# Six chunks' scores on 40 rows instead of 104, a mask moved to GpSimd, and a new order of the first steps: an mLSTM with a feed-forward on one core

## The chip, the cores and the metric

The kernel runs on one NeuronCore of one Trainium2 chip. TensorE multiplies matrices, VectorE (DVE), ScalarE (ACT) and GpSimd (POOL) do elementwise work, and SyncE (SP) issues nearly all DMAs. The metric is the device time of one execution in microseconds: 464.96 us is the median of three runs (464.77 to 465.43).

## The reference

An mLSTM over 768 time steps for 4 batches and 8 heads of width 40, then a feed-forward of width 2048 over the heads' joined outputs (3072 tokens of 320):

```python
for t in range(S):
    m_new = np.maximum(f_gate[:, :, t] + m, i_gate[:, :, t])
    f_stab, i_stab = np.exp(f_gate[:, :, t] + m - m_new), np.exp(i_gate[:, :, t] - m_new)
    C = f_stab * C + i_stab * outer(vt, kt);  n = f_stab * n + i_stab * kt;  m = m_new
    y[:, :, t] = sigmoid(o_gate[:, :, t]) * (C @ qt) / np.maximum(np.abs(n @ qt), 1.0)
h = x @ w_in
out = (np.maximum(h, 0) + alpha * np.minimum(h, 0)) @ w_out
```

## The kernel before, in words

The 768 steps of a batch are six chunks of 128 tokens; chunk n = 6b + c is chunk c of batch b, 24 in all. Inside a chunk the recurrence is written as attention: scores K Q^T of each head (keys on the partitions, queries along the row) times a decay matrix E that is zero where the key comes after the query, times the values; and what came before the chunk enters through a state C, which is multiplied by a decay gamB and added to for each chunk (`update`, lines 183 to 223). Two chunks are one group g of 256 tokens, 12 groups, on which the feed-forward runs: `up_steps` (lines 749 to 787) multiplies by w_in, `down` (789 to 813) by w_out, in eight pairs fp of 128-column blocks. The result of a pair is split in a high part (`gh`, ScalarE) and a low part (`gl`); the token letters of a pair are U R S G K, where VectorE computes into PSUM and makes the low part, or V r s g N, where GpSimd makes the low part (line 785).

The weights come as float64. Each block is loaded (token letter d), scaled by ScalarE (s), joined from its two words by VectorE (j), and split in a high part by ScalarE (h, H) and a low part by VectorE (l, L) or by GpSimd (p, P), line 891. The third bit group comes either by ScalarE (x, line 865) with a longer join on VectorE (line 877), or by a shift on VectorE (y, line 871) with another join (line 879).

The first six chunks (batch 0, `n < NDIR`) take a road of their own. q and k are loaded by token, transposed on TensorE (`transposed`, line 266: two heads to a block, head 2p on partitions 0 to 39 and head 2p+1 on 64 to 103, with zeros between) and copied from PSUM by ScalarE. k goes to a padded tile of two halves (`padded_copy`, lines 322 and 323): the half of the even heads has zeros on the partitions from 64, that of the odd heads on those below 64, so that the scores (line 1097) may contract over all 104 partitions:

```python
nc.tensor.matmul(ps[:, sl], qk[n][1][:R, par, sl], qk[n][0][:R, sl], start=True, stop=True)
```

`par` is the parity of the head; a call makes the four heads of one parity, in float32, which the trace shows as two records (a weight load and a matmul each) per instruction. The decays of chunks 0 to 3 come through PSUM: `barred` (line 100) first writes a triangle of large negative numbers with a 512-column bfloat16 matmul, `spread` (1052) or `spread_later` (1064) adds the rows of L to it, and ScalarE takes the exponential (1080). Chunks 4 and 5 load L by DMA, and GpSimd zeroes the upper triangle of E with a select (line 489). VectorE multiplies scores and E (line 1101).

The order of all this is written out by hand: ORDER (line 686) is a string of 414 tokens, each a step with its instructions, and `pin` (line 944) holds every engine's queue to that order. After ORDER's last token Z0 (group 0's output is copied out at 104 us) a repeating PATTERN issues the rest; steps done in ORDER are left out there. A warm token is that many bfloat16 matmuls of 256 columns whose output nobody reads. PSUM tiles named by `psa` come from two tags, "a" and "b", of two buffers each, given in turn.

Of the kernel before, what the change touches and what calls it, by code (L numbers as in the profile page):

```python
# [17 lines left out]
def kernel(ctx: ExitStack, tc: tile.TileContext, q, k, v, i_gate, f_gate, o_gate, w_in, w_out, alpha, out):  # L18
# [286 lines left out]
    kpads = []  # L305

    def padded_tiles():


        for K in kpads:  # L310
            nc.gpsimd.memset(K[64:R, 0], 0.0)
            nc.gpsimd.memset(K[:64, 1], 0.0)

# [102 lines left out]
    def gated_steps(n, hv):  # L416
# [21 lines left out]
        if b == 0:  # L438
            nc.vector.scalar_tensor_tensor(out=sg, in0=sg, scalar=1.0, in1=rb, op0=ALU.add, op1=ALU.mult)
        else:  # L440
            nc.gpsimd.tensor_tensor(sg, sg, rb, ALU.mult)
# [38 lines left out]
    def decays_of(n, par, Lb):  # L480
# [3 lines left out]
        for p in range(NPR):  # L484
            h = 2 * p + par
            nc.scalar.activation(  # L486
                E[:, p * P : (p + 1) * P], Lb[:, h], AF.Exp, bias=bT[:, c, b * H + h : b * H + h + 1]
            )
        nc.gpsimd.affine_select(
# [166 lines left out]
    def first_stacks():  # L656
# [23 lines left out]
    XNP = range(2, NBF)  # L680
    KDP = range(1, 24)
    CP = range(6, 24)
    OBA = range(0)
    WIDE = 3 * VA
    ORDER = """warm18 kfz alT lf0z warm2 warm2 i00d i00s sca0 lf0a lf0b dq0 L0 sp01 qT0 dq1 alC li0 bj0 wt0 bTt kT0 i00x qc0 kc0 ewj
        i01d sca1 bTc ex01 sp00 sc00 qT1 wTt eeL wTc qc1 wd0 li1 lf1a lf1b kT1 sc01 i00j ex00 kc1 eTt Cz eTc sp11 ex11
        dv0 wg01 i01s wd1 L1 um0 uc0 i01x lpa um1 sp10 wg00 gma gmd ex10 i01j i00h fm1 ft1 sc11 do0 sc10 wg10 bj1 wtl
        blt ewl blc i00p o0d o0s r0d o0x gmm gmc r0s r0x v0 wg11 lpb lpc lpd uc1 dq2 qT2 o2d gr0 wlt og1 warm2 wlc r0j
        i11d lpe o0j i01h i01p gg0 qc2 dq3 gx0 gp0 kT2 v1 eel elt elc sp21 kc2 sc21 dL r0H ta1 gr1 gg1 sp20 ex21 qT3
        wg21 i10d dv1 r0h gx1 gp1 r0p r0L ex20 wd2 sc20 wg20 qc3 x0 x1 xa0 xd0 dq4 fm2 wd3 xa1 xd1 i10s F0 ft2 o2s o2y  # L690
        sp31 o0h ex31 kT3 o2j o2h i10y i10j um2 U00 o0l V01 kc3 R00 i11s uc2 i11y i11j o2l do1 i10h i10l sp30 r01 qT4
        qc4 ex30 S00 v2 sc31 i20d i20s ta2 gr2 i20x wg31 o1d og2 gg2 gx2 kT4 i20j kc4 sc30 wg30 G00 K00 i21d fm3 ft3
        s01 i20h o1s i20p i11h i11p o1x r2d o1j i21s i21x sc41 v3 um3 i21j uc3 ta3 dL4 U02 V03 r2s r2y o3d gr3 sc40
        ex41 fm4 R02 dq5 o1h o1l o4d g01 r2j N01 qT5 i21h i21p o3s S02 o3x G02 K02 dL5 wg41 i31d ft4 D00 wd4 dq6 o3j
        qc5 dv2 r2h r2p r03 ex40 o4s r2H D01 o4x gg3 s03 o3h o4j gx3 o5d gp3 wg40 i30d V04 r04 s04 dv3 o4h V05 gp2 x2
        x3 xa2 xd2 o6d do2 wd6 kT5 g04 r2P g03 o3l xa3 r05 o4l s05 v4 xd3 kc5 i31s ta4 N03 N04 i31y i31j i30s o5s o5x
        F1 V10 gr4 r10 um4 uc4 dL6 i30x um6 U11 ex50 R11 o5j s10 uc6 S11 ex51 g10 i31h dL7 i31p sc50 N10 i30j dq7 wg50
        U12 fm5 ft5 o5h sc51 wg51 v5 o7d R12 S12 ta5 D10 G11 K11 o6s o6x gr5 og3 gg5 G12 gx5 gg4 D11 K12 D12 i30h i30l
        gx4 U13 gp5 D02 tp0 do3 U06 o7s gp4 o5l o6j vp0 R13 tp1 g05 S13 G13 N05 K13 o7x o6h D13 vp1 o7j U07 tp2 tp3
        R06 S06 R07 x4 x5 xa5 xd5 D03 D04 D05 S07 o7h o7l G06 K06 o6l D06 xa4 xd4 G07 K07 D07 Z0"""  # L700
# [36 lines left out]
    class FeedForward:  # L737

        def __init__(self, g):
            self.g, self.x, self.done, self.named = g, x_tiles.pop(g), [], 0  # L740
# [4 lines left out]
        def up(self):  # L745
            for step in self.up_steps(self.g < 2):
                pass

        def up_steps(self, split=True):
            g, fp = self.g, self.named  # L750
            self.named += 1
# [34 lines left out]
            self.done.append((gh, gl))  # L786
# [179 lines left out]
    def first_group():  # L966
# [79 lines left out]
        def spread(n, par):  # L1046

            pb = psa(f"pb{n}_{par}")
            barred(pb)
            for p in range(NPR):  # L1050
# [3 lines left out]
                    start=False, stop=p == NPR - 1  # L1054
# [3 lines left out]
        def spread_later(n, par):  # L1058

            pb = psa(f"pb{n}_{par}")  # L1060
            barred(pb)
            for p in range(NPR):
# [3 lines left out]
                    LP[:, n % GC * P : (n % GC + 1) * P], start=False, stop=p == NPR - 1,  # L1066
# [5 lines left out]
        def decay(n, par):  # L1072
# [10 lines left out]
            E[n, par] = e  # L1083
# [4 lines left out]
        def scores(n, par):  # L1088
            if n >= GC:
                ps = psa(f"pS{n}_{par}")  # L1090
            elif n * par == 0:
# [275 lines left out]
```

## Time and profile before

| | us |
|---|---|
| median of three runs (range) | 464.96 (464.77 to 465.43) |
| the profiled execution, whole | 465.35 |
| its span, first to last instruction | 463.6 |
| TensorE busy in the first 80 us | 72.75 |
| TensorE busy from 80 to 450 us | 370.00 of 370 |
| DVE, ACT, POOL busy in the first 80 us | 65.93, 66.71, 45.05 |

The profiled execution has 1.7 us outside its span. Busy time of TensorE counts a matmul from its start to its modelled end, while the next may have begun: where matmuls follow each other, the step from start to start is shorter than the duration shown, and a short wait can lie inside busy time.

### The profile page before, as it was taken

The page shows a single profiled execution, that of the slowest core. Times are in us where ns is not written, and L with a number is a line of the kernel's source. Part 1 is how long each engine was busy: PE and PEld are TensorE (multiplying, and loading weights), DVE is VectorE, ACT ScalarE, POOL GpSimd, SP SyncE. Part 2 cuts the span into 40 slices and gives each one's busy share as a digit, 9 for nine tenths or more (in the row PEclk, how much of TensorE's full clock was granted, in tenths as well). Part 3 has the DMA queues.
Part 4 walks back from the last instruction along what each step waited for, and adds up shares of the span by engine and source line. Part 5 has one row for each costly group of instructions (what it writes and reads, how often), then busy time and mean ns, then how long its engine had stood idle before and what let it go on. Part 6 is the DMA issues. An engine that isn't in the chain of part 4 may idle for free.

```text
span 463.6 us, 11813 instructions
## 1 busy us (share of the span) xinstructions
PE 452.8 (98%) x4366; PEld 442.0 (95%) x4366; DVE 329.8 (71%) x692; ACT 315.0 (68%) x707; POOL 308.4 (67%) x377
## 2 busy tenths in 40 slices
PE   8989989999999999999999999999999999999996
PEld 6879978999999999999999999999999999999996
DVE  4989998747776787886875887886776786764321
ACT  4899898676857858758856958757857858423331
POOL 8551674854698697588888598588888686324231
PEclk9999999999999999999999999999999999999999
DMA  9999994869775775888997686688796463020000
GB/s 184 177 221 252 277 252 118 175 122 190 151 182 147 138 184 160 137 174 173 158 187 176 122 197 168 133 166 180 153 206 156 107 154 90 1 84 15 28 2 28
DMA packets 186306, 68.67 MB, mean 148 GB/s; under 512 B 150234, under 2 KB 178506, under 8 KB 186250
## 3 DMA queue, kind: packets, MB, share of 16 engines
q1 hardware_dynamic: 186170, 67.83, 67.2%
q8 instruction: 34, 0.56, 0.5%
q14 instruction: 22, 0.18, 0.2%
q10 hardware_dynamic: 80, 0.11, 0.1%
HBM read 40.44 MB, written 7.57 MB: 104 GB/s over the span
## 4 chain that ended last, share of the span: by engine, by line
PE 83%; DVE 5%; DMA 5%; SPq 3%; ACT 3%; issue 1%; ACTq 0%; DVEq 0%
PE po L796 36%; PE ph L759 5%; PE ph L765 5%; PE ph L762 5%; PE ph L760 5%; PE ph L761 5%; PE ph L764 4%; PE ph L763 4%; PE ph L766 4%; PE pH L377 4%; PE pS L515 4%; DMA wi<-in_moe_w_in_dram 2%; DMA wr<-in_moe_w_in_dram 2%; PE pI L403 1%; PE pu L203 1%; DMA qn<-in_q_dram 1%
## 5 line engine op out<-in xcount | busy, mean ns | idle before, releaser
L785 POOL TENSOR_TENSOR gl<-g,gh 128x512 fp32r<-128x512 f32 x77 | 100.5, 1306 | 42.9 <-ACT gh L783 39.6
L796 PE MATMUL po<-OH,gh 128*128 128x320 f32 x368 | 110.7, 312 | 0.0
L796 PE MATMUL po<-OL,gh 128*128 128x320 f32 x368 | 109.3, 309 | 0.0
L769 ACT ACTIVATE g<-ph 128x512 f32<-128x512 f32 x96 | 57.1, 596 | 58.2 <-PE ph L766 56.0
L774 DVE SCALAR_TENSOR_TENSOR g<-g,oma,ph 128x256 f32<-128x256 f32 x156 | 66.8, 469 | 32.7 <-ACT g L769 32.3
L796 PEld LDWEIGHTS po<-OL,gh 128*128 128x128 f32 x368 | 69.2, 188 | 0.1
L796 PEld LDWEIGHTS po<-OH,gh 128*128 128x128 f32 x368 | 69.1, 188 | 0.0
L796 PE MATMUL po<-OH,gl 128*128 128x320 f32 x368 | 69.0, 309 | 0.0
L759 PE MATMUL ph<-XH,WH 128*128 128x256 f32 x192 | 57.2, 298 | 1.1 <-ACT wo L865 0.7
L796 PEld LDWEIGHTS po<-OH,gl 128*128 128x128 f32 x368 | 57.9, 188 | 0.0
L764 PE MATMUL ph<-XL,WH 128*128 128x256 f32 x192 | 54.3, 283 | 0.9 <-DVE XL L623 0.9
L765 PE MATMUL ph<-XL,WH 128*128 128x256 f32 x192 | 54.3, 283 | 0.0
L762 PE MATMUL ph<-XH,WL 128*128 128x256 f32 x192 | 54.3, 283 | 0.0
L760 PE MATMUL ph<-XH,WH 128*128 128x256 f32 x192 | 54.1, 282 | 0.0
L761 PE MATMUL ph<-XH,WL 128*128 128x256 f32 x192 | 54.1, 282 | 0.0
L364 ACT CAST E<-pS 128x512 bf16<-128x512 f32 x72 | 41.6, 582 | 18.0 <-DVE pS L361 14.0
L763 PE MATMUL ph<-XH,W 128*128 128x256 f32 x192 | 53.4, 278 | 0.2 <-POOL W L891 0.2
L766 PE MATMUL ph<-XL,W 128*128 128x256 f32 x192 | 53.4, 278 | 0.0
L783 ACT CAST gh<-g 128x512 fp32r<-128x512 f32 x77 | 46.5, 618 | 9.1 <-DVE g L774 6.6
L486 ACT ACTIVATE E<-Lb,bT 128x128 f32<-128x128 f32 x160 | 50.0, 392 | 0.0
L361 DVE TENSOR_TENSOR pS<-pS,E 128x512 f32<-128x512 f32 x36 | 24.8, 690 | 29.6 <-PE pS L515 26.2
L759 PEld LDWEIGHTS ph<-XH,WH 128*128 128x128 f32 x192 | 36.1, 188 | 2.0 <-ACT wo L865 0.9
(197 smaller groups left out, 1123.2 us busy)
## 6 DMA issues: line engine op xcount, KB each, us to landing
Lb<-L_d SPq DMA_DIRECT2D x20, 512.0 KB
wo<-in_moe_w_out_dram SPq DMA_DIRECT2D x8, 640.0 KB
wi<-in_moe_w_in_dram SPq DMA_DIRECT2D x8, 512.0 KB
qn<-in_q_dram SPq DMA_DIRECT2D x24, 160.0 KB
kn<-in_k_dram SPq DMA_DIRECT2D x24, 160.0 KB
va<-in_v_dram SPq DMA_DIRECT2D x24, 160.0 KB
og<-in_o_gate_dram SPq DMA_DIRECT2D x24, 160.0 KB
out_dram<-ob SPq DMA_DIRECT2D x11, 320.0 KB
```

The costliest lines, as they stand in the source:

```text
L759: nc.tensor.matmul(dst, WH[half][:, 0, hs], XH[:, 0], start=True, stop=False)
L760: nc.tensor.matmul(dst, WH[half][:, 1, hs], XH[:, 1], start=False, stop=False)
L761: nc.tensor.matmul(dst, WL[half][:, 0, hs], XH[:, 0], start=False, stop=False)
L762: nc.tensor.matmul(dst, WL[half][:, 1, hs], XH[:, 1], start=False, stop=False)
L763: nc.tensor.matmul(dst, W2[:, fs], X2, start=False, stop=False)
L764: nc.tensor.matmul(dst, WH[half][:, 0, hs], XL[:, 0], start=False, stop=False)
L765: nc.tensor.matmul(dst, WH[half][:, 1, hs], XL[:, 1], start=False, stop=False)
L766: nc.tensor.matmul(dst, W2[:, fs], X2L, start=False, stop=True)
L769: nc.scalar.activation(gt, ph, AF.Relu, scale=-1.0)
L774: nc.vector.scalar_tensor_tensor(out=y[:, e], in0=gt[:, e], scalar=oma[:, f : f + 1], in1=ph[:, e], op0=ALU.mult, op1=ALU.add)
L785: (nc.vector if split else nc.gpsimd).tensor_tensor(gl, y, gh.bitcast(F32), ALU.subtract)
L796: nc.tensor.matmul(po[j], x[:, e, j * P : (j + 1) * P], W[f // NB][:, f % NB], **ends)
```

## The change

- `scores(n)` makes both parities in one call. Each head is a matmul over its own 40 partitions (0 to 39 or 64 to 103), even and odd heads in turn, into two PSUM tiles. k is then copied unpadded, in one ScalarE copy instead of two, and the four memsets of the padded tiles (token kfz) are gone.
- Chunk 3 is taken out of the barred chunks (BAR): its spread begins the PSUM group itself, and GpSimd's select masks E.
- CP: for chunks 1 to 4, GpSimd multiplies C by its decay, in one instruction of 104x336, where VectorE did it in two. KDP: chunk 1's weighted keys go to VectorE. XNP: chunk 1's last gating product goes to GpSimd and chunk 2's to VectorE. OGP is empty: its steps (tokens ga) issue nothing, and `gated_steps` is as before.
- ORDER is new throughout, with 419 tokens. By its tokens: four low parts of w_out go from VectorE to GpSimd (ol 8 to 4, op 0 to 4) and one of the w_in rest (rL to rP); five blocks go from x to y (two of w_in, three of w_out); four feed-forward pairs go from U to V (00, 07, 11, 13); warm2 three times is now warm3 three times. The DMAs are the same, in another order (q of chunk 0 is now first on SP).
- The first 50 PSUM tiles without a tag take theirs from a written list.

```diff
+    first_turns = list("abababaaabbbaabbabbbaaababbaababababbabaaaabbbbbaba")
     def psa(name, tag=None):
+        if tag is None and first_turns:
+            tag = first_turns.pop(0)
...
-    XNP = range(2, NBF)
-    KDP = range(1, 24)
-    CP = range(6, 24)
+    XNP = (1, *range(3, 6))
+    KDP = range(2, 24)
+    CP = range(1, 24)
+    OGP = range(0)
+    BAR = range(3)
...
-    ORDER = """warm18 kfz alT lf0z warm2 warm2 i00d i00s sca0 lf0a lf0b dq0 L0 sp01 qT0 dq1 alC li0 bj0 wt0 bTt kT0 i00x qc0 kc0 ewj
+    ORDER = """dq0 warm18 qT0 i00d dq1 lf0z alT sca0 qc0 sca1 lf0a lf0b li0 alC i00s do0 L0 kT0 i00x warm3 eeL sp01 bj0 bTt
...
-        R06 S06 R07 x4 x5 xa5 xd5 D03 D04 D05 S07 o7h o7l G06 K06 o6l D06 xa4 xd4 G07 K07 D07 Z0"""
+        D05 o6l K06 xd5 g07 xa4 N07 o7l D06 xd4 D07 Z0"""
...
             if j == 0:
-                qk[n] = sb.tile([P, 512], F32, tag="qf", name=f"qf{n}"), padded(n)
-                copy(qk[n][j][:R], pq[:R])
-            else:
-                padded_copy(qk[n][j], pq)
+                K = sb.tile([P, 2, 512], F32, tag="kS", name=f"kf{n}", bufs=2)[:, 0]
+                qk[n] = sb.tile([P, 512], F32, tag="qf", name=f"qf{n}"), K
+            copy(qk[n][j][:R], pq[:R])
...
-            barred(pb)
+            if n in BAR:
+                barred(pb)
...
-            E[n, par] = e
+            E[n, par] = e if n in BAR else causal(e)
...
+            for h in range(H):
+                p, par = divmod(h, 2)
+                sl, r = slice(p * P, (p + 1) * P), slice(64 * par, 64 * par + D)
+                nc.tensor.matmul(pS[n, par][:, sl], qk[n][1][r, sl], qk[n][0][r, sl], start=True, stop=True)
...
-                steps[f"sc{n}{par}"] = lambda par=par: scores(n, par)
+                steps[f"sc{n}{par}"] = lambda: (n, 0) in pS or scores(n)
```

## Rows read from the trace of the kernel before

**Rows 1.** Busy time by stage: the window in us, its length, then busy us (and instructions) of PE, PE's weight loads, DVE, ACT and POOL, the granted TensorE clock, the DMA engines' mean busy share and GB/s.

```profile
0.00:80.00 80.00, 72.75 (x655) 66.17 (x656) 65.93 (x137) 66.71 (x148) 45.05 (x65) 1.00 0.93 211
80.00:450.00 370.00, 370.00 (x3644) 366.04 (x3644) 261.33 (x551) 245.08 (x555) 260.81 (x311) 1.00 0.65 139
...
30.00:40.00 10.00, 9.64 (x96) 8.69 (x95) 8.88 (x20) 9.40 (x24) 3.43 (x4) 1.00 0.84 159
...
70.00:80.00 10.00, 8.94 (x77) 8.42 (x72) 8.15 (x18) 8.15 (x20) 4.85 (x6) 1.00 0.36 105
```

**Rows 2.** What TensorE waited for, whole span, the longest waits behind the one for the constants at the start: its line, the releaser's engine, tile and line, us in total, times, longest.

```profile
PE ph L764 <- DVE XL L623: 0.9, 1, 0.9
PE pb L100 <- DVE xn L443: 0.8, 1, 0.8
PE pH L337 <- DVE E L1101: 0.8, 2, 0.6
PE ph L759 <- ACT wo L865: 0.7, 1, 0.7
PE ps_gw L1022 <- ACT E L1080: 0.5, 1, 0.5
PE ps_ge L1022 <- ACT g_WH L1227: 0.4, 1, 0.4
```

**Rows 3.** The chain that ended last, in order of time: start us, us, what; one DMA issue on SP (SPq) at its start, and its two longest transfers of weights.

```profile
2.20 0.58 SPq L106
...
14.25 8.14 DMA wr<-in_moe_w_in_dram
...
37.39 8.24 DMA wi<-in_moe_w_in_dram
```

**Rows 4.** TensorE's timeline from 14 to 22 us: start us, us from the first start to the last end, engine, line, operation, tiles, shape, and how many records follow each other.

```profile
13.63 0.39 PE L100 MATMUL pb<-later,ident 128*128 128x512 bf16 x1
13.86 1.05 PE L1052 MATMUL pb<-g_L,ident 128*128 128x128 f32 x8
14.84 0.81 PE L203 MATMUL pu<-va,kd 128*40 128x42 f32 x32
15.59 0.39 PE L100 MATMUL pb<-later,ident 128*128 128x512 bf16 x1
```

**Rows 5.** TensorE's timeline from 9 to 11.5 us (the scores of one parity, eight records), and line 1097 as a whole: durations ns min/median/max, first and last start.

```profile
9.77 1.06 PE L1097 MATMUL pS<-qf,kf 104*128 104x128 f32 x8
...
L1097 PE MATMUL pS<-qf,kf x96: 272/275/377, 9.8 to 77.4; 104*128 104x128 f32 x96
```

**Rows 6.** Line 203, the state's update, as a whole: the same columns.

```profile
L203 PE MATMUL pu<-va,kd x320: 199/202/233, 14.8 to 379.3; 128*40 128x42 f32 x160
```

**Rows 7.** Groups of DVE in the first 80 us, shapes apart: line, operation, out<-in, shapes, count | busy us, mean ns | idle before.

```profile
L877 DVE SCALAR_TENSOR_TENSOR t_wo<-t_wo,wo 128x640 uint32<-128x640 uint32 x5 | 5.7, 1140 | 0.4 <-ACT wo L865 0.2 <-POOL xn L443 0.2
L877 DVE SCALAR_TENSOR_TENSOR t_wi<-t_wi,wi 128x512 uint32<-128x512 uint32 x5 | 4.6, 923 | 0.0
L891 DVE TENSOR_TENSOR OL<-t_wo,OH 128x640 fp32r<-128x640 f32 x5 | 4.0, 810 | 0.0
L221 DVE TENSOR_TENSOR C<-C,gamB 40x168 f32<-40x168 f32 x8 | 2.5, 318 | 0.1
L879 DVE SCALAR_TENSOR_TENSOR t_wi<-wi,t_wi 128x512 uint32<-128x512 uint32 x3 | 2.1, 692 | 0.1
L871 DVE TENSOR_SCALAR t_wi<-t_wi 128x512 uint32<-128x512 uint32 x3 | 1.7, 574 | 0.0
L785 DVE TENSOR_TENSOR gl<-ph,gh 128x512 fp32r<-128x512 f32 x2 | 1.4, 686 | 0.7 <-ACT gh L783 0.7
L879 DVE SCALAR_TENSOR_TENSOR t_wo<-wo,t_wo 128x640 uint32<-128x640 uint32 x1 | 0.8, 828 | 0.0
L871 DVE TENSOR_SCALAR t_wo<-t_wo 128x640 uint32<-128x640 uint32 x1 | 0.5, 494 | 0.4 <-ACT t_wo L855 0.4
```

**Rows 8.** The same view of ACT.

```profile
L323 ACT COPY kf<-pqk 40x512 f32<-40x512 f32 x6 | 3.5, 581 | 0.1
L865 ACT ACTIVATE wo<-wo 128x640 uint32<-128x640 uint32 x5 | 4.0, 802 | 0.0
L865 ACT ACTIVATE wi<-wi 128x512 uint32<-128x512 uint32 x5 | 3.4, 676 | 0.0
```

**Rows 9.** The same view of POOL.

```profile
L891 POOL TENSOR_TENSOR WL<-t_wi,WH 128x512 fp32r<-128x512 f32 x6 | 8.2, 1371 | 1.6 <-ACT WH L887 1.5
L785 POOL TENSOR_TENSOR gl<-g,gh 128x512 fp32r<-128x512 f32 x3 | 4.9, 1660 | 2.3 <-ACT gh L783 2.3
L172 POOL TENSOR_TENSOR kd<-kn,wT 128x320 f32<-128x320 f32 x5 | 3.5, 719 | 0.1
L489 POOL TENSOR_SCALAR_AFFINE_SELECT E<-E 128x512 f32<-128x512 f32 x4 | 2.7, 679 | 6.8 <-ACT E L486 4.1 <-DVE C L221 2.3 <-POOL W L891 0.4
L443 POOL TENSOR_TENSOR xn<-T,og 128x320 f32<-128x320 f32 x2 | 1.9, 972 | 10.5 <-DVE og L439 10.5
```

**Rows 10.** The spread of one instruction's duration on DVE, by line: ns min/median/max, first and last start us.

```profile
L877 DVE SCALAR_TENSOR_TENSOR t_wo<-t_wo,wo x7: 826/1291/1583, 24.7 to 90.6; 128x640 uint32<-128x640 uint32 x7
L439 DVE SCALAR_TENSOR_TENSOR og<-og,r x6: 483/492/1553, 25.9 to 82.3; 128x320 f32<-128x320 f32 x6
L891 DVE TENSOR_TENSOR OL<-t_wo,OH x8: 774/818/1446, 37.2 to 99.8; 128x640 fp32r<-128x640 f32 x8
```

More of the change, by code (lines that the diff above doesn't have):

```diff
@@ L143, in open_gate_last, with open_gate_early @@
         nc.vector.tensor_scalar(og, og, 1.0, None, ALU.add)
+    def open_gate_early(n):
+        if n in OGP:
+            sg = o_tiles[0][:, n]
+            nc.gpsimd.tensor_scalar(sg, sg, 1.0, None, ALU.add)
     def open_gate(b, c0=0, c1=NC):
@@ L303, in shifted @@
         chunk[n] = (Q, K, None)
[L305 to L312, printed above, removed]
     def zero_states():
@@ L438, in gated_steps @@
         if b == 0:
-            nc.vector.scalar_tensor_tensor(out=sg, in0=sg, scalar=1.0, in1=rb, op0=ALU.add, op1=ALU.mult)
+            if n in OGP:
+                nc.gpsimd.tensor_tensor(sg, sg, rb, ALU.mult)
+            else:
+                nc.vector.scalar_tensor_tensor(out=sg, in0=sg, scalar=1.0, in1=rb, op0=ALU.add, op1=ALU.mult)
         else:
@@ L488, in decays_of, with causal @@
             )
+        return causal(E)
+    def causal(E):
         nc.gpsimd.affine_select(
@@ L739, in __init__ @@
         def __init__(self, g):
-            self.g, self.x, self.done, self.named = g, x_tiles.pop(g), [], 0
+            self.g, self.x, self.done = g, x_tiles.pop(g), {}
             if g == 1:
@@ L743, in __init__, with up_steps @@
                 self.po = [ps_a.tile([P, 512], F32, tag="b", name=f"po{g}_{j}")[:, :DM] for j in range(GC)]
[L745 to L751, printed above, removed]
+        def up_steps(self, fp, split):
+            g = self.g
             XH, XL, X2, X2L = self.x
@@ L785, in up_steps @@
             (nc.vector if split else nc.gpsimd).tensor_tensor(gl, y, gh.bitcast(F32), ALU.subtract)
-            self.done.append((gh, gl))
+            self.done[fp] = gh, gl
             yield
@@ L1027, in by_token @@
             yield
-        for j in range(2):
-            kpads.append(sb.tile([P, 2, 512], F32, tag="kS", name=f"kf{j}", bufs=2))
         qk = {}
@@ L1053, in spread @@
                     pb[:, p * P : (p + 1) * P], ident[:, h : h + 1].broadcast_to([P, P]), L_all[:, n * P : (n + 1) * P],
-                    start=False, stop=p == NPR - 1
+                    start=n not in BAR, stop=n not in BAR or p == NPR - 1
                 )
@@ L1060, in spread_later @@
             pb = psa(f"pb{n}_{par}")
-            barred(pb)
+            if n in BAR:
+                barred(pb)
             for p in range(NPR):
@@ L1065, in spread_later @@
                     pb[:, p * P : (p + 1) * P], pick[:, h : h + 1].broadcast_to([3 * BH, P]),
-                    LP[:, n % GC * P : (n % GC + 1) * P], start=False, stop=p == NPR - 1,
+                    LP[:, n % GC * P : (n % GC + 1) * P], start=n not in BAR, stop=n not in BAR or p == NPR - 1,
                 )
@@ L1082, in decay, with scores @@
                 )
-            E[n, par] = e
+            E[n, par] = e if n in BAR else causal(e)
             yield
         pS = {}
[L1088 to L1091, printed above, removed]
-                ps = ps_h.tile([P, 512], F32, tag="h", name=f"pS{n}_{par}")
-            else:
-                ps = ps_o.tile([P, 512], F32, tag="o1", name=f"pS{n}_{par}")
-            for p in range(NPR):
-                sl = slice(p * P, (p + 1) * P)
-                nc.tensor.matmul(ps[:, sl], qk[n][1][:R, par, sl], qk[n][0][:R, sl], start=True, stop=True)
-            pS[n, par] = ps
+        def scores(n):
+            for par in range(2):
+                if n >= GC:
+                    pS[n, par] = psa(f"pS{n}_{par}")
+                elif n * par == 0:
+                    pS[n, par] = ps_h.tile([P, 512], F32, tag="h", name=f"pS{n}_{par}")
+                else:
+                    pS[n, par] = ps_o.tile([P, 512], F32, tag="o1", name=f"pS{n}_{par}")
+            for h in range(H):
+                p, par = divmod(h, 2)
+                sl, r = slice(p * P, (p + 1) * P), slice(64 * par, 64 * par + D)
+                nc.tensor.matmul(pS[n, par][:, sl], qk[n][1][r, sl], qk[n][0][r, sl], start=True, stop=True)
         def weigh(n, par):
@@ L1245, in chunk_steps @@
                 add(f"fm{n} ft{n}", lazily(lambda: state_part(n)))
+            steps[f"ga{n}"] = lambda: open_gate_early(n)
             add(f"gr{n} gg{n} gx{n} gp{n}", lazily(lambda: gated_steps(n, got["T" if n else "h", n])))
@@ L1306, in named_ffn @@
                 for tokens, split in (("URSGK", True), ("VrsgN", False)):
-                    add(" ".join(f"{x}{g}{fp}" for x in tokens), lazily(lambda split=split: ffs[g].up_steps(split)))
+                    add(" ".join(f"{x}{g}{fp}" for x in tokens), lazily(lambda fp=fp, split=split: ffs[g].up_steps(fp, split)))
                 steps[f"D{g}{fp}"] = lambda fp=fp: ffs[g].down(fp)
```

36 lines of the change are left out of this document (16 added, 20 removed).

## The prediction

> **What bounds the kernel now.** The busy time by stage comes first [rows 1]. From 80 to 450 us TensorE is busy for 370.00 of 370 us, with DVE, ACT and POOL at 66 to 71%: there TensorE's own instructions are the time. In the first 80 us it is busy for 72.75 and idle for 7.25, with DVE at 65.93, ACT at 66.71 and the DMA engines at a mean share of 0.93; POOL has 35 us free. So the end comes at: all the work of TensorE, plus the time in which it stands still in the first 80 us. The change can act on these two alone, and nothing that it does on another engine behind 80 us is worth anything.
>
> What TensorE waits for is read next [rows 2]. No single wait is over 0.9 us. Those for DVE (0.9, 0.8, 0.8) make 2.5 us, those for ACT (0.7, 0.5, 0.4) 1.6 us: together 4.1 of the 7.25. The chain that ended last [rows 3] shows what is under them: two transfers of weights stand in it with 8.14 and 8.24 us, so that in part of the first 46 us neither DVE nor ACT sets the pace but the loads. Those are all issued again.
>
> **TensorE's work, part by part.** Scores: eight records of one parity take 1.06 us from first start to last end, and one lasts 0.275 [rows 5], so they follow each other in (1.06 - 0.275) / 7 = 0.112 us. A chunk has 16 records, 1.79 us; six chunks 10.8 us. The change keeps the 96 records and their 128 columns; what it can save is time in which an even head's records run beside an odd head's. Does this chip do that? The trace has no matmul on part of the rows beside another. It has the nearest kin, the state's update, whose even heads write to partitions 0 to 39 and odd ones to 64 to 103: 32 records in 0.81 us, each 0.202 long [rows 4, 6], follow each other in (0.81 - 0.20) / 31 = 0.0196 us. At the scores' rate per column, 42 columns would take 0.112 x 42 / 128 = 0.037 us. The update goes twice as fast, so its heads do run in pairs. If rows behave as columns, a chunk's 16 records in the order even, even, odd, odd need 8.5 slots of 0.112 (the first and the last stand alone): 0.95 us, which saves 0.84 a chunk and 5.0 us in six.
>
> The update also shows what it costs to enter and leave such a mode [rows 4]. The last record before it starts at 13.86 + 1.05 - 0.28 = 14.63, the update at 14.84: 0.21 instead of 0.11. Its own last record starts at 14.84 + 0.81 - 0.20 = 15.45, the next matmul at 15.59: 0.14 instead of 0.02. So a block pays 0.10 + 0.12, and six blocks 1.3 us. The scores give 5.0 - 1.3 = 3.7; I take -3.6, as a feed-forward matmul behind a block may pay a little more. The ends are +1.3 (no pairs, the switches alone) and -5.0 (no switches). The Trainium skill's page "TensorEngine Tiling (Array Packing)", section "Tiling Modes", says that changing the tiling mode drains TensorE; that is the 0.22 us just read, and by it the change pays six drains that the kernel before did not have.
>
> Bars: two matmuls of 512 columns go, with 13.86 - 13.63 = 0.23 us from start to start [rows 4]: -0.46. Warm matmuls: three more of 256 columns, half a bar each: 3 x 0.115 = +0.35; where they fill a wait they cost nothing, so between 0 and that. TensorE's work: -3.6 - 0.46 + 0.35 = -3.7 us.
>
> **What the other engines lose or get in the first stage** (some of it falls behind 80 us, where it counts for nothing). DVE: C's decay, 8 x 0.318 = -2.5; four low parts of w_out, 4 x 0.81 = -3.2; one of the rest, 0.69 by the 512 columns of line 785 = -0.7; four pairs from U to V, 4 x 0.686 = -2.7 [rows 7]. Five blocks from x to y cost it, for w_in, 0.574 + 0.692 - 0.923 = 0.34 twice, and for w_out 0.494 + 0.828 - 1.140 = 0.18 three times: +1.2. Chunk 1's keys: +0.5, as a 128x320 product of two tiles (the shortest of line 439 is 0.483 [rows 10]). The two gating products change places. Sum -7.4 us of 65.9. ACT: six copies of k less, 6 x 0.581 = -3.5, and five third bit groups less, 2 x 0.676 + 3 x 0.802 = -3.8 [rows 8]: -7.3 of 66.7. POOL gets four low parts of 640 columns (1.371 x 640/512 = 1.71 each), one of 512 (1.3), four low parts of pairs (1.66 each), four decays of C (0.72 to 0.97 each by 128x320 products; I take 0.85) and two selects (0.68) [rows 9]: 6.9 + 1.3 + 6.6 + 3.4 + 1.4 = 19.6, less chunk 1's keys (0.7) and four memsets at the start. About 17 us more on 45: some 62 of 80, so it has room.
>
> C's decay now stands ahead of the addition of the new part on another engine: DVE's addition waits for POOL, and behind it stand the next chunk's row scaling and product. As the decay needs only the state before, it can run while the update's matmuls do; I price it at nothing, and at up to 0.8 us a chunk (an instruction of POOL that it meets) if POOL is late. Both parities' scores now want two of four PSUM buffers at once: also nothing, and at most a wait like the 0.8 us of line 100 [rows 2].
>
> The loads keep their sizes and their queue, SP, and change places. At the head, q and k of chunk 0 were issued behind the first block of w_in; now q goes ahead of it. That puts the block back by one issue of some 0.58 us [rows 3], and TensorE's first transpose, now straight behind the 18 warm matmuls, holds the scans' transposes behind it if q is late. Further back, loads of weights, v and gates change places by a few issues each. I price each at nothing, since what they feed is not the next thing in its engine's queue, and at one issue, 0.6 us, for the first block if ScalarE is there early; what the moves do together lies in the idle time below.
>
> **DVE and POOL disturb each other.** Line 877's instruction on the same shape takes 0.826 to 1.583 us, line 439's 0.483 to 1.553, line 891's 0.774 to 1.446 [rows 10], all with two inputs in SBUF. The Trainium skill's page "SBUF — State Buffer", section "Who interferes with whom", has a rule that speaks against this change: a DVE instruction with two SBUF inputs and a GpSimd instruction that reads SBUF hold each other up, the later one for all of the earlier. The spreads agree with it. By the rows alone: with 17/45 more POOL time, a hold-up of up to 0.76 us (1.583 - 0.826) is met more often; I allow 2 us of the 7.4, so that DVE keeps -5.
>
> **TensorE's idle time.** With DVE and ACT 5 to 7 us lighter, the 4.1 us of waits for them may shrink; against that TensorE has 3.7 us less to do, mostly in the stage, and where a load sets the pace this comes back as idle time. I take the balance at -0.8: from -4.1 (all these waits go) to +3.7 (all is given back).
>
> **Sum.** 465.35 - 3.7 - 0.8 = 460.85 for an execution like the profiled one. That lies 0.39 above the median of the runs shown, so the forecast is 460.5 us.
>
> **The rivals.**
> - *The waits go too.* For: DVE and ACT lose 11% each where they were 83% busy. Against: the transfers in [rows 3]. 464.96 - 3.7 - 4.1 = 457.2.
> - *The loads keep the pace.* For: DMA share 0.93 over the stage, only 0.84 from 30 to 40 us and 0.36 from 70 to 80 [rows 1]. Against: TensorE idles 7.25 us and not more, so that loads do not hold it for most of the stage. Then only what is saved behind the last load counts, the scores of chunk 5 (the last records start at 77.4 us [rows 5]): 3.6 / 6 = 0.6, and 464.4.
> - *Rows do not pair.* The change would not do what it says: +1.3 - 0.46 + 0.35 = +1.2 in work, -0.8 in waits: 465.4. Against it speaks the update's rate.
> - *Slower: POOL's new work holds DVE up.* 15 instructions are new on POOL (4 + 1 + 4 + 4 + 2). If 12 of them hold a DVE instruction for 0.76 us, DVE gets 9.1 and loses 7.4: +1.7 in a stage that it then sets, and TensorE's saving is idle time: 466.7. It decides from 10 hold-ups on (7.4 / 0.76). For: of line 877's seven instructions on w_out the middle one already takes 1.291 [rows 10]. Against: part of what moves away from DVE (the low parts of line 891) is itself of the kind that is held up.
>
> **How the numbers follow.** The forecast has 0.55 (458.5 to 462.5), the waits that go too 0.18, the loads 0.08, no pairs 0.06, POOL's hold-up 0.13. A difference under 0.2% (0.93 us) cannot be told from none: the loads and no pairs lie within it, so faster 0.73, same 0.14, slower 0.13. For 8 in 10 the range leaves out the slower case and the far half of the fastest: 456 to 465.5.
>
> **What would show it.** In the changed profile: line 1097's successor as 96 records with 40 rows, 16 of them in about 0.95 + 0.28 us from first start to last end (right) or in 2 us (no pairs); a gap of 0.1 us on both sides of each block; six matmuls of line 100's kind instead of eight; DVE and ACT some 5 to 7 us lighter and POOL some 17 heavier by the end of the first 110 us; TensorE idle for 6 to 7 us in the first 75 us and at 100% from there. The prediction is wrong if idle time in the stage is over 10 us (loads or POOL), if line 877's median rises beyond 1.4 us with TensorE waiting on DVE, or if TensorE saturates as late as before.

## The result, and the profile after

The changed kernel takes 468.10 us (median of four runs, 468.08 to 468.18), the one before 464.87 us in the same comparison: a ratio of 1.0068, with a 95% interval from 1.0054 to 1.0082. It is slower by 3.2 us, where 4.4 us less was forecast, and lies outside the range.

The first view is the busy time by stage of the changed kernel, with the columns of [rows 1]; three shorter windows around one event follow.

```profile
0.00:80.00 80.00, 68.91 (x644) 61.48 (x645) 62.64 (x119) 57.84 (x133) 53.32 (x71) 0.98 0.88 200
80.00:450.00 370.00, 368.61 (x3631) 364.26 (x3630) 262.92 (x556) 247.16 (x557) 265.76 (x314) 1.00 0.65 141
...
55.00:62.40 7.40, 4.90 (x36) 4.40 (x34) 6.86 (x13) 4.11 (x9) 5.28 (x7) 1.00 1.03 320
62.40:65.80 3.40, 3.18 (x15) 3.21 (x16) 2.74 (x5) 3.35 (x9) 1.02 (x3) 0.50 0.55 64
65.80:80.00 14.20, 14.20 (x150) 13.70 (x149) 11.94 (x22) 10.82 (x27) 11.26 (x12) 1.00 0.56 142
```

The whole execution with the same columns, the kernel before first:

```profile
0.00:463.60 463.60, 452.83 (x4366) 442.04 (x4366) 329.80 (x692) 315.04 (x707) 308.45 (x377) 1.00 0.68 148
```

```profile
0.00:466.40 466.40, 450.79 (x4367) 438.75 (x4367) 328.97 (x681) 309.12 (x696) 324.21 (x387) 1.00 0.67 147
```

TensorE stands idle for 11.09 us of the first 80 (7.25 before), and for 1.4 us more behind 80, where it had none. Over the whole span its busy time falls by 2.0 us and its idle time grows from 10.8 to 15.6 us; together these are the 2.8 us between the two spans. The DMA share is 0.88 against 0.93, so the loads do not press harder. In the first 80 us ACT does 8.9 us less and DVE 3.3 us less, but the changed kernel is late there (119 instructions of DVE instead of 137). Over the whole execution ACT does 5.9 us less and DVE only 0.8, although the change takes 7 us from each. POOL does 15.8 us more. And for 3.4 us, behind a wait of TensorE, its granted clock is 0.50, that is 1.2 instead of 2.4 GHz.

The scores themselves do what the update's rows promised. The next fence is TensorE's timeline with one chunk's block, and line 1095 as a whole (what was line 1097 in [rows 5]).

```profile
12.22 1.16 PE L1095 MATMUL pS<-qf,kf 40*128 40x128 f32 x16
13.31 0.65 PE L274 MATMUL pqk<-ident,qn 128*104 128x128 f32 x4
...
L1095 PE MATMUL pS<-qf,kf x96: 272/272/373, 12.2 to 76.6; 40*128 40x128 f32 x96
```

From the block's first start to the next instruction's start the 16 records take 13.31 - 12.22 = 1.09 us, entry and exit partly in it, where they took 1.8.

The waits of the changed kernel, against [rows 2] (the columns as there; TensorE's over the whole span, the two others over the first 90 us):

```profile
PE p L604 <- DVE T L400: 2.5, 1, 2.5
PE pH L329 <- DVE E L1098: 1.4, 1, 1.4
PE pS L1095 <- DVE C L230: 0.9, 1, 0.9
...
DVE C L230 <- POOL C L218: 4.1, 3, 2.2
...
ACT qf L1035 <- PE pqk L274: 6.4, 3, 2.8
ACT gh L780 <- DVE ph L771: 3.3, 1, 3.3
ACT t_wi L852 <- POOL OL L888: 2.0, 2, 1.3
```

```profile
ACT qf L1039 <- PE pqk L266: 1.0, 1, 1.0
```

Each engine now waits for another: TensorE for DVE, DVE for the decays that were moved to POOL, ACT for POOL's low parts and, for 6.4 us, for TensorE's transposes of q. The last line is the kernel before, where that wait was 1.0 us. Of the 6.4 us, 2.8 lie at the very start, where ACT waited 2.7 us for the first block of w_in before; the other 3.6 stand against the 1.0.

Last, DVE and POOL side by side from 76 to 82 us (start, us, engine, line, operation), and DVE's small gating instruction by line:

```profile
77.22 0.64 DVE L1098 TENSOR_TENSOR E<-pS,E 128x512 f32<-128x512 f32 x1
77.77 3.49 DVE L868 TENSOR_SCALAR t_wo<-t_wo 128x640 uint32<-128x640 uint32 x1
...
77.61 0.82 POOL L259 TENSOR_TENSOR C<-cw,C 40x336 bf16<-40x336 f32 x1 [0.58 <-ACT C L257]
78.40 1.27 POOL L782 TENSOR_TENSOR gg<-g,gg 128x512 fp32r<-128x512 f32 x1
79.63 1.28 POOL L782 TENSOR_TENSOR gl<-g,gh 128x512 fp32r<-128x512 f32 x1
...
L422 DVE SCALAR_TENSOR_TENSOR r<-T x5: 166/587/1844, 27.9 to 87.7; 128x8 f32<-128x8 f32 x5
```

A shift of 0.49 us lasts 3.49 us: it ends at 81.26, and three POOL instructions that follow each other without a gap end at 80.91. A 128x8 instruction of 0.17 us lasts up to 1.84: it starts at 56.47 us and ends at 58.32, and the second of two POOL instructions in a row ends at 58.29. In both cases DVE's instruction ends just behind the last of a chain of POOL's.

### The profile page after: what moved, and what is told of

Read it like the earlier page. It is cut to its first block, busy times and chain, and to the rows that moved or that the text cites. A ratio compares the mean times of both kernels' runs of the same rounds, so it can differ in the third digit from the quotient of the medians.

```text
span 466.4 us, 11800 instructions
## 1 busy us (share of the span) xinstructions
PE 450.8 (97%) x4367; PEld 438.8 (94%) x4367; DVE 329.0 (71%) x681; ACT 309.1 (66%) x696; POOL 324.2 (70%) x387
## 4 chain that ended last, share of the span: by engine, by line
PE 86%; DVE 5%; ACT 3%; POOL 3%; issue 1%; DMA 1%; DVEq 0%; POOLq 0%
PE po L793 35%; PE ph L756 5%; PE ph L759 5%; PE ph L762 5%; PE ph L761 4%; PE ph L757 4%; PE ph L758 4%; PE ph L763 4%; PE ph L760 4%; PE pH L369 4%; PE pS L514 4%; PE pH L329 2%; PE pu L211 1%; PE pI L395 1%; POOL WL L888 1%; PE pb L1047 1%
## 5 line engine op out<-in xcount | busy, mean ns | idle before, releaser
L782 POOL TENSOR_TENSOR gl<-g,gh 128x512 fp32r<-128x512 f32 x79 | 103.1, 1307 | 38.3 <-ACT gh L780 35.0
L771 DVE SCALAR_TENSOR_TENSOR g<-g,oma,ph 128x256 f32<-128x256 f32 x164 | 70.2, 469 | 33.8 <-ACT g L766 33.2
L780 ACT CAST gh<-g 128x512 fp32r<-128x512 f32 x79 | 47.8, 617 | 9.0 <-DVE g L771 6.5
L759 PEld LDWEIGHTS ph<-XH,WL 128*128 128x128 f32 x192 | 36.8, 192 | 0.7 <-POOL WL L888 0.7
```

Of the source, the lines that this page charges most:

```text
L759: nc.tensor.matmul(dst, WL[half][:, 1, hs], XH[:, 1], start=False, stop=False)
L771: nc.vector.scalar_tensor_tensor(out=y[:, e], in0=gt[:, e], scalar=oma[:, f : f + 1], in1=ph[:, e], op0=ALU.mult, op1=ALU.add)
L782: (nc.vector if split else nc.gpsimd).tensor_tensor(gl, y, gh.bitcast(F32), ALU.subtract)
```

## The experiments

All times are medians, each beside runs of the kernel before on the same chip (464.8 to 465.1 in all five groups, so that differences between runs of two groups are good to some 0.3 us); the last column is the ratio to it with its 95% interval.

| run | us | ratio |
|---|---|---|
| e1 rows in pairs alone, in the kernel before | 469.0 | 1.008 (1.005 to 1.011) |
| e2 changed, POOL's work back | 468.3 | 1.007 (1.005 to 1.009) |
| e3 changed, POOL's low parts write only | 466.2 | 1.002 (1.001 to 1.003) |
| e4 before, POOL's low parts write only | 464.8 | 0.999 (0.998 to 1.000) |
| e5 e1's places, 104 rows | 467.4 | 1.005 (1.003 to 1.007) |
| e6 e1, waits filled | 465.8 | 1.002 (1.000 to 1.004) |
| e7 changed, rows unpaired | 470.0 | 1.010 (1.009 to 1.012) |
| e8 changed, 104 rows | 472.5 | 1.017 (1.014 to 1.019) |
| e9 changed, waits filled | 468.1 | 1.007 (1.005 to 1.008) |
| e10 changed, decays back | 466.5 | 1.004 (1.002 to 1.005) |
| e11 pairs at the first place, in the kernel before | 466.4 | 1.003 (1.002 to 1.005) |
| e12 changed, low parts back | 466.2 | 1.003 (1.002 to 1.004) |
| e13 changed, decays and low parts back | 467.6 | 1.005 (1.004 to 1.007) |
| e14 changed, feed-forward pairs back | 468.4 | 1.007 (1.005 to 1.008) |
| e15 changed, shifts back | 468.8 | 1.008 (1.006 to 1.009) |
| e16 e11 with warm matmuls | 466.1 | 1.003 (1.001 to 1.004) |
| e17 the new order alone | 474.5 | 1.021 (1.019 to 1.022) |
| e18 before, two low parts on POOL | 465.5 | 1.001 (1.000 to 1.002) |

**The order alone (e17, e8, e7).** These three and the changed kernel make a ladder, and it is the main result. e17 keeps the new order and the work of before. Some of its lines against the changed kernel:

```diff
-    XNP = (1, *range(3, 6))
-    KDP = range(2, 24)
-    CP = range(1, 24)
+    XNP = range(2, NBF)
+    KDP = range(1, 24)
+    CP = range(6, 24)
...
-    BAR = range(3)
+    BAR = range(4)
```

The scores go over 104 rows again, and ORDER has the new places with the tokens of before: o0l o1l o2l o4l r0L, the pairs U00 U07 U13, and x or y for each block as before. The order here also takes in the places of the loads, both parities' scores in one place, and the written list of PSUM tags, which e17 keeps.

> The new order with the work of the kernel before: 104-row scores, chunk 3 barred, decays, keys, gating products, low parts, the forms of the weight blocks and the feed-forward pairs as before (pair 11 alone stays with GpSimd). If the order itself is what costs: 470 to 474, about as much as e8. If the moved work was the loss: 465 to 467.

474.45 us: the order theory's number, half a microsecond above its range. The new order with the old work costs 474.45 - 464.77 = 9.7 us. Where it falls behind is read from the busy time by stage; the first three rows are of the kernel before, the last three of e17 (both have the same instructions, but for one feed-forward pair, two low parts of w_in that change engines against each other, and three warm matmuls):

```profile
0.00:30.00 30.00, 26.17 (x228) 22.24 (x228) 21.36 (x47) 21.84 (x51) 19.21 (x39) 1.00 1.02 207
30.00:60.00 30.00, 29.27 (x266) 27.68 (x265) 27.61 (x54) 27.86 (x62) 13.97 (x13) 1.00 0.98 232
60.00:90.00 30.00, 27.31 (x239) 26.25 (x238) 23.93 (x50) 24.07 (x51) 19.51 (x23) 1.00 0.74 182
```

```profile
0.00:30.00 30.00, 25.61 (x212) 21.33 (x212) 18.99 (x42) 19.14 (x44) 17.68 (x37) 1.00 1.11 210
30.00:60.00 30.00, 26.57 (x241) 24.04 (x239) 21.76 (x48) 24.48 (x55) 8.72 (x10) 1.00 0.76 175
60.00:90.00 30.00, 26.68 (x225) 25.34 (x224) 26.00 (x47) 23.44 (x50) 18.62 (x19) 0.94 0.70 186
```

At 60 us DVE has done 40.75 us of work instead of 48.97, ACT 43.62 instead of 49.70, TensorE 453 records instead of 494. The kernel before keeps DVE and ACT over 90% busy from 30 to 60 us; e17 has them at 73 and 82%. Its waits in the first 90 us name several links:

```profile
ACT qf L1052 <- PE pqk L274: 8.2, 4, 3.0
ACT XH L633 <- DVE XL L638: 1.7, 1, 1.7
...
DVE t_wr L884 <- ACT t_wr L868: 2.9, 1, 2.9
DVE OL L904 <- ACT OH L900: 2.6, 2, 2.5
...
PE p L620 <- DVE T L416: 1.4, 1, 1.4
```

The largest is ACT's for the transposes of q. Its first two waits, what stands ahead of the second in TensorE's queue, and ACT's wait at the start of the kernel before:

```profile
5.97 0.59 ACT L1052 COPY qf<-pqk 104x512 f32<-104x512 f32 x1 [2.96 <-PE pqk L274]
14.67 0.58 ACT L1052 COPY qf<-pqk 104x512 f32<-104x512 f32 x1 [3.00 <-PE pqk L274]
...
12.14 2.05 PE L1114 MATMUL pS<-qf,kf 104*128 104x128 f32 x16
14.03 0.60 PE L274 MATMUL pqk<-ident,qn 128*104 128x128 f32 x4
```

```profile
5.68 0.67 ACT L855 ACTIVATE t_wi<-wi 128x512 f32<-128x512 f32 x1 [2.67 <-DMA wi<-in_moe_w_in_dram]
```

The first wait takes the place of one that the kernel before had too. The other 5.2 us stand against 1.0 in the kernel before: in TensorE's queue the scores or the values of an older chunk stand ahead of the transposes, ACT stands still, and what it makes for DVE comes late. How much of the 9.7 us this link makes was not tried; that the order makes them is measured.

e8 keeps order and moved work, with the scores over 104 rows; e7 keeps the 40 rows but issues the even heads first and then the odd ones:

```diff
-            for h in range(H):
+            for h in (0, 2, 4, 6, 1, 3, 5, 7):
```

> The changed kernel with its order, but the scores over 104 padded rows as before (two copies of k on ScalarE and the memsets of the padded tiles back). Give-back theory: 466.5 to 469.5, with TensorE at the full clock throughout; what the order and the moved work cost, some 3 us, is all there. If TensorE's saved time is worth its length: 471 to 473.

> The changed kernel with the four even heads of a chunk ahead of the four odd ones, so that only one pair of records in 16 can overlap: TensorE has some 4.7 us (6 chunks x 7 slots x 0.112) more to do, all else is the same. Give-back theory: the waits shrink by as much, the time is 466 to 469. If TensorE's saved time is worth its length: 471.5 to 473.

472.54 and 469.95 us. e8 goes against the give-back theory, e7 lies between the two. A block of e7 still overlaps in part:

```profile
12.02 1.71 PE L1095 MATMUL pS<-qf,kf 40*128 40x128 f32 x16
```

It is 0.55 us longer than the changed kernel's, 3.3 us in six. So the moved work gives 474.45 - 472.54 = 1.9 us, and the scores on 40 rows, with ScalarE's single copy of k and without the memsets, 472.54 - 468.10 = 4.4 us, of which 1.9 come from taking even and odd heads in turn instead of all even ones first. The order takes 9.7, the work gives back 6.3. These steps hold in this sequence alone: taken out of the changed kernel one by one, two parts of the moved work cost time (e10, e12 below). The old order with all of the new work was not run.

**The pairs in the kernel before (e1, e5, e6, e11, e16).** e1 takes the new `scores` into the kernel before, with both parities where the later one stood (kfz gone, three weighings behind the scores); e5 has these places with 104 rows; e6 is e1 with matmuls in its waits; e11 has both parities where the first stood and no weighing moved; e16 is e11 with ten more warm matmuls.

```diff
-... sp21 kc2 sc21 dL ... wg21 i10d dv1 ... wd2 sc20 wg20 ...
+... sp21 kc2 dL ... i10d dv1 ... wd2 sc20 wg21 wg20 ...            (e1, e5, e6)
+... sp21 kc2 sc21 dL ... wg21 i10d dv1 ... wd2 sc20 wg20 ...       (e11, e16: sc21 makes both)
+... warm8 v0 ... warm14 v3 ... hold14 U11 ... hold8 v5 ...         (e6)
+... warm6 elt ... warm4 sp21 ...                                   (e16)
```

> The kernel before with the scores by 40 rows and in pairs, nothing else of the change: its own order, its own division between VectorE and GpSimd; a chunk's scores are issued where the later parity's were, and the weighing of three parities follows them. If the pairing is worth on TensorE what the trace after shows (96 records at a mean step of 0.056 us instead of 0.112, less six changes of mode), the time falls by 2.5 to 4.5 us, to 460.5 to 462.5. If the loads or VectorE set the pace of the first 80 us, it falls by 1 us at most (464 or more).

> The control of e1_rows_alone: the same places of the scores and weighings as there, but the scores again over 104 padded rows, one after the other. Give-back theory (TensorE does not set the pace of the first stage; what the pairs save turns into waits, and a TensorE with less to do is granted half the clock for a while at these waits): no stretch at half clock before the end, time 464.5 to 466, so better than with the pairs. Place theory (the moved scores and weighings are what cost 4 us in e1): 467.5 to 470, or more than e1.

> e1_rows_alone with matmuls whose output nobody reads put into the four waits ahead of its three stretches at half clock: 8 and 14 warm matmuls ahead of the values of chunks 0 and 3, and 14 and 8 of 192 columns (into unused columns of a PSUM bank) ahead of pair 11 and of the values of chunk 5. Give-back theory: the clock stays at 2.4 GHz and the time falls by 2.5 to 4.5 us to 464.5 to 466.5, hardly below the kernel before. Place theory: the clock may stay up, but the time is within 1.5 us of 469.

e1, 469.01 us, is neither expected case: slower than before by 3.9 with less work. Its profile shows what happened; the windows are cut where the granted clock changes:

```profile
0.00:20.80 20.80, 17.93 (x161) 14.49 (x162) 14.00 (x30) 12.51 (x32) 14.50 (x32) 1.00 1.04 194
20.80:24.20 3.40, 3.40 (x18) 3.39 (x18) 1.91 (x7) 2.86 (x7) 0.62 (x2) 0.50 0.71 151
24.20:48.10 23.90, 20.44 (x195) 17.77 (x194) 21.27 (x46) 20.06 (x47) 7.89 (x10) 1.00 1.02 234
48.10:51.50 3.40, 3.40 (x30) 3.09 (x29) 3.17 (x8) 3.26 (x8) 1.15 (x2) 0.50 1.13 239
51.50:82.20 30.70, 27.18 (x251) 25.58 (x251) 25.25 (x51) 24.25 (x51) 18.68 (x19) 1.00 0.75 193
82.20:85.60 3.40, 3.40 (x17) 3.40 (x16) 1.38 (x4) 1.65 (x3) 0.65 (x1) 0.51 1.04 210
```

Three stretches of 3.4 us at 1.2 GHz, each behind a block of pairs and a wait of TensorE of 0.7 to 1.8 us; only 18 and 17 of TensorE's records fit in the first and the last. e5, with the same places and TensorE kept busier by unpaired scores, shows the full clock up to its last matmuls and takes 467.43, at the lower edge of the place theory; e6, with the waits filled, shows the same and takes 465.81, within the give-back theory. So the moved scores and weighings cost 2.4 us (e5 against before), the pairs without the clock give back 1.6 of it (e6 against e5), and the half clock costs 3.2 (e1 against e6). Single runs of e6 spread from 464.7 to 468.6, so the last two numbers are good to a microsecond at best.

> The kernel before with the pairs, but a chunk's scores issued where its first parity's were, and every weighing where it was; PSUM tags from a list. Against e1 and e5 no weighing is late. If the 2.4 us that e5 lost come from the late scores and weighings, this gives 462.5 to 465.5 when the clock stays up, and up to 467 with one or two falls. If the pairs bring falls of the clock anyway that cost more than they save: 466 to 469.

> e11_rows_at_first_place with 10 more warm matmuls (1.1 us) in TensorE's waits at 25 to 27 us, ahead of its one stretch at half clock. If that stretch costs its 1.6 us: 464.5 to 465.3, as good as the kernel before and no better, since VectorE and ScalarE set the pace. If TensorE's saved 4 us were worth their length once the clock is up: 461 to 463.

466.41 and 466.06 us. e11's profile has one stretch at half clock (28.8 to 32.2 us), and its time fits both of its cases; e16's profile has none, and its time fits neither of its own, 0.8 us above the first. e16's profiled execution (464.91 us) is the fastest of ten, which go up to 467.81, so it shows no gain over the kernel before. Six blocks of 1.09 instead of 1.8 us save TensorE some 4 us, and neither median shows any of it: in the order of before TensorE's length alone does not set the time of the first stage.

**The half clock in the changed kernel (e9).** Matmuls that nobody reads in the wait ahead of the stretch at 62.4 us, and in the one at 81 us:

```diff
-... o4y o3j x2 ...    ... v5 ...
+... o4y o3j hold24 x2 ...    ... hold12 v5 ...
```

> The changed kernel with matmuls whose output nobody reads (192 columns, into unused columns of a PSUM bank) in its two longest waits: 24 ahead of the transposes of chunk 2's result, just before the clock fell, and 12 ahead of the values of chunk 5. If the half clock costs what its rows show (3.41 us at half, some 16 matmuls at 0.21 instead of 0.12: about 1.6 us), the time falls by 1 to 2 us to 466 to 467. If VectorE or GpSimd, not TensorE, sets the pace there too: 467.7 to 468.5 at the full clock.

468.07 us at the full clock: nothing. Two of the changed kernel's four runs had a mean clock of 0.996 and two of 1.000, and all lie between 468.08 and 468.18. What e9 gains behind 62.4 us it loses in a new wait of 1.0 us for ACT at 70.5 us, and the values of chunk 5 start at 82.93 us instead of 82.98, behind the same instruction of DVE. The fall does not need the pairs either: e17, with scores over 104 rows, shows it too (0.94 in its row from 60 to 90 us).

**POOL and DVE (e2, e3, e4, e10, e12 to e15, e18).** In e3 and e4 POOL reads one column and otherwise only writes:

```diff
-            (engine or nc.vector).tensor_tensor(l, t, h.bitcast(F32), ALU.subtract)
+            nc.gpsimd.tensor_tensor(l[first], t[first], h[first], ALU.subtract)
+            for _ in range(3):
+                nc.gpsimd.memset(l[rest].bitcast(F32), 0.0)
```

> The changed kernel; every low part that GpSimd makes in the first two groups and of the weights is left out but for one column, and three memsets take its place (about 1.5 us where the subtraction takes 1.3), so that GpSimd is as busy, but reads nothing from SBUF in that time. Hold-up theory: VectorE's long instances (1.84 us for a 128x8 instruction, 3.49 us for a shift) are gone, and the time falls by 3 us or more, below 465.2. Order theory: the time stays within 1 us of 468.1.

> The same replacement in the kernel before: its GpSimd low parts of the first two groups and of the weights as three memsets with one column computed. Hold-up theory: VectorE's hold-ups before were 7.5 us where those after are 13.5, so the gain is smaller than in the changed kernel: 0.5 to 2.5 us, to 462.5 to 464.5. Order theory: within 1 us of 465.

466.17 and 464.77 us. Whole executions of e3 and e4, with the columns of [rows 1]:

```profile
0.00:464.70 464.70, 451.56 (x4367) 439.25 (x4367) 321.55 (x681) 308.58 (x696) 334.31 (x465) 1.00 0.68 148
```

```profile
0.00:462.90 462.90, 453.85 (x4366) 442.62 (x4366) 324.18 (x692) 315.46 (x707) 313.73 (x428) 1.00 0.70 148
```

The changed kernel gains 1.9 us, the one before 0.3. DVE's busy time falls by 7.4 us in the changed kernel and by 5.6 in the one before, with the same instructions: POOL's reads hold DVE up, and cost about 2 us of the changed kernel's time. POOL is busier in e3 than in the changed kernel (70.3 us of the first 90 instead of 58.9), so it is not its length. Theory and size differ: 3 us or more were expected, and the rest of the loss stays; in the kernel before the time stays as the order theory said.

DVE's shifts and joins of w_out, in the changed kernel and then in e3 (durations ns min/median/max, first and last start):

```profile
L868 DVE TENSOR_SCALAR t_wo<-t_wo x4: 486/740/3490, 22.3 to 96.7; 128x640 uint32<-128x640 uint32 x4
L876 DVE SCALAR_TENSOR_TENSOR t_wo<-wo,t_wo x4: 812/1043/1790, 24.1 to 97.6; 128x640 uint32<-128x640 uint32 x4
```

```profile
L878 DVE TENSOR_SCALAR t_wo<-t_wo x4: 489/746/1362, 22.3 to 94.9; 128x640 uint32<-128x640 uint32 x4
L886 DVE SCALAR_TENSOR_TENSOR t_wo<-wo,t_wo x4: 806/816/826, 24.1 to 95.8; 128x640 uint32<-128x640 uint32 x4
```

The joins, with two inputs in SBUF, take at most 0.83 us in e3 where they took up to 1.79. The Trainium skill's rule that was weighed ahead of the result ("SBUF — State Buffer", "Who interferes with whom") speaks of a DVE instruction with two SBUF inputs beside a GpSimd instruction that reads SBUF, and the joins agree with it. The low parts that DVE makes of w_out, with two inputs too, still reach 1.45 us in e3, where POOL's other reads are left; the shift that was held for 3.49 us has one input and is not a case of that rule as it was weighed. That shift was held through three POOL instructions, longer than any one of them lasts.

> The changed kernel with its new order, but five low parts of weights, three of the four feed-forward pairs and the decays of chunks 1 to 4 again on VectorE. Hold-up theory (GpSimd's added work holds VectorE's instructions up): VectorE gets 8 us of instructions more and still is earlier, the time falls to 464 to 466.5. Order theory (the new places of the steps make the waits, whoever does the work): VectorE is busier and the time is 468 to 471.

> The changed kernel with the state's decays of chunks 1 to 4 on VectorE again (8 instructions of 0.32 us) and nothing else undone. GpSimd theory (GpSimd's queue, in order, became what the first stage waits for: VectorE waited 2.8 us for its decays): the time falls by 1 to 3 us to 465 to 467. If VectorE's load counts for as much: 467.5 to 469.

> The changed kernel with its five moved low parts of weights on VectorE again (0.7 to 0.8 us each there, 1.3 to 1.6 on GpSimd). GpSimd theory: ScalarE's 2.9 us of waits for GpSimd's low parts go, and the time falls by 1 to 2.5 us to 465.5 to 467. If VectorE's load counts for as much: 467.5 to 469.

> The changed kernel with the decays of chunks 1 to 4 and the five low parts of weights on VectorE, the feed-forward pairs left on GpSimd. If GpSimd's queue is the whole loss: both gains add to some 3.4 us, 464.5 to 465.3. If VectorE takes over as the one that is late (it gets 6.5 us back), the second gain is lost: 466 to 468.

```diff
-    CP = range(1, 24)            (e2, e10, e13)
+    CP = range(6, 24)
-... o0p o1p o2p o4p r0P ...      (e2, e12, e13)
+... o0l o1l o2l o4l r0L ...
-... V00 V07 V13 ...              (e2, e14)
+... U00 U07 U13 ...
-... i01y i21y o0y o4y o5y ...    (e15)
+... i01x i21x o0x o4x o5x ...
```

The decays alone back on DVE give 1.6 us (466.48), the low parts alone 1.9 (466.24), as the GpSimd theory had it; both together give only 0.5 (467.60), both with the feed-forward pairs nothing (468.33, the order theory's case). One row of each profile shows where the engines stand (busy time of the first 90 us; e10, e12 and then e13):

```profile
0.00:90.00 90.00, 78.51 (x717) 70.16 (x718) 76.37 (x146) 65.24 (x146) 57.60 (x73) 1.00 0.88 201
```

```profile
0.00:90.00 90.00, 79.78 (x719) 71.18 (x720) 75.53 (x144) 65.59 (x147) 52.70 (x72) 1.00 0.87 202
```

```profile
0.00:90.00 90.00, 77.88 (x712) 69.31 (x713) 76.60 (x151) 64.39 (x144) 48.28 (x67) 1.00 0.87 200
```

With both back TensorE has done least by 90 us (77.88 us) and DVE most (76.60), which fits the expected case that DVE takes over as the late one. But DVE's busy time does not rank the three runs: e10 has 76.37 us and is as fast as e12 with 75.53. Why the two gains do not add is not shown.

> The changed kernel with only the three feed-forward pairs 00, 07 and 13 back in the form in which VectorE makes the low part. If e2's bad time comes from these pairs (VectorE then works in PSUM and holds TensorE's buffer until the low part is done): 468.5 to 471. If they are GpSimd's load like the others: 466 to 467.5.

> The changed kernel with the five blocks (01, 21 of w_in; 0, 4, 5 of w_out) back on ScalarE's form (0.7 to 0.8 us more on ScalarE each, no shift on VectorE, whose single-input shift took 3.49 us behind three GpSimd instructions once). Hold-up theory: 466 to 467.5. If ScalarE's load counts for as much: 467.7 to 469.5.

468.35 and 468.77: the feed-forward pairs are neutral, between their two cases, and these five shifts on DVE were right in this order, though one shift was held for 3 us; ScalarE's form costs 0.7 more. (The change moves nine blocks from x to y and four the other way, so that five is its net; e15 gives back five of the nine.)

> The kernel before with two low parts of w_out (blocks 0 and 2, VectorE at 37 and 40 us) on GpSimd, which stands idle for 10 us there, nothing else. If VectorE's queue sets the pace between 30 and 60 us and is not held up in return: 463.5 to 464.6. If the 1.7 us on GpSimd come back as waits for its later instructions or as hold-ups: 465 to 466.5.

```diff
-... o0l ... o2l ...
+... o0p ... o2p ...
```

465.46 us, 0.7 more than the kernel before: even where POOL stands idle for 10 us, two low parts moved to it gain nothing. No kernel here beats the one before by more than its interval.

## Why the prediction was wrong

- *TensorE bounds from 80 us on, and its idle time in the first 80 decides.* Right as a frame: from 80 us on TensorE is busy for 368.6 of 370 us, and idle 3.8 us longer in the first stage.
- *TensorE's idle time, -0.8, with +3.7 as its end.* This is the step that failed. It measured +4.8 us over the whole execution (10.8 to 15.6), 3.8 of them in the first 80 us. The balance counted how many microseconds each engine loses, and did not follow which queue each moved step now stands behind. In the sum the new order of the engines' steps has no term: the words "I price each at nothing" are for the moved loads, C's decay stands at nothing too, and "what the moves do together" was left to this balance, whose upper end is what TensorE saves, as if nothing else could add waits. In its place e17 shows that the new order with the old work costs 9.7 us, with DVE 8.2 us of work behind at 60 us. A sign stood in the rows: the kernel before has DVE and ACT at over 90% from 30 to 60 us, so that a step put behind a longer one has little room. Which moved step costs how much stays open.
- *Scores, -3.6.* Right as work of TensorE: a block takes 1.09 us to the next start where 0.95 + 0.22 was worked out. The sum counts it as time in full, and that does not follow: taking the heads in turn saves TensorE 3.3 us and 1.9 us of time (e7), and in the order and at the places of before the pairs gain nothing (e11, e16). The 4.4 us of e8 contain six copies on ACT as well. All of TensorE's work, -3.7 in the sum, shows as -2.0 us of busy time, with 3.4 us at half clock among it.
- *DVE, -7.4 and 2 of it lost to hold-ups.* Mis-sized: over the whole execution DVE's busy time falls by 0.8 us. With POOL's low parts only written, the changed kernel's DVE is 2.6 us below the one before (e3, e4), so that these reads take 1.8 of the missing 6.6 us. The rest may lie in instructions that last longer beside POOL's other work and in the shift's form, which was priced from a few instances; that is not shown.
- *ACT, -7.3, and POOL, about +17.* Near: 5.9 us less and 15.8 us more over the whole execution.
- *C's decay on POOL, at nothing.* Wrong: DVE waited 4.1 us for it, and e10 gives 1.6 us back.
- *The slower rival* (POOL's work holds DVE up, 466.7, at 0.13) names something that is there, but in time it is worth about 2 us (e3), while the order costs 9.7 and the new work and the new scores give 6.3 back. That its number lies within 1.4 us of the result is luck. That the order itself could be worse was no rival at all.
- *The loads keep the pace.* No: the DMA share fell to 0.88, and no wait of TensorE for a load is over 0.2 us.
- *The signs of being wrong.* Two of the three came: TensorE stood idle for over 10 us in the stage, and its last wait there ends at 83.0 us, where it ended at 78.5. The first was put down to loads or POOL; e17 has 10.8 us of idle time in its first 80 us without POOL's new work. The third did not come: the joins of line 877 have a median of 0.99 us on w_out.
- *TensorE's clock* was not in the prediction. It did not decide here (e9), though it did in e1.

## What to carry to other kernels

In this kernel's first stage, where three engines are each over 80% busy, the sum of what each engine loses said little, and the place of each step in its queue said more. So a new order must be priced link by link (what stands ahead of this transpose now, who waits for it), or measured alone with the old work, as e17 did. Measure a new form of an operation and a new order apart: here the form gave 4.4 us and the order took 9.7. Compare two orders at equal work and not at equal time, as the later one has done less of it by then. When work moves to POOL, whose reads hold DVE up (e3), look at DVE's longest instances afterwards, not at its instruction count.

## What was not expected of the hardware

- Matmuls on rows 0 to 39 and 64 to 103 in turn run in pairs: 16 float32 records in 1.09 us instead of 1.8, with six more changes of mode.
- With pairs in the order of before (e1), the clock fell to 1.2 GHz three times for 3.4 us, behind waits of 0.7 to 1.8 us; the same order without pairs (e5) has waits of up to 1.5 us and stayed at 2.4 GHz. The fall cost about 3 us there. In the changed kernel one fall cost nothing (e9), and in its order it comes without pairs too (e17).
- DVE can be held by a chain of POOL instructions: 3.49 us for a shift of 0.49, 1.84 us for 128x8 elements.
